# Decode attention on one core: q in one load, shared norms and stores, and the last V loads in pieces

## The chip, the cores and the metric

The kernel runs on one core of a Trainium2 chip. The metric is the device time in microseconds (us), lower is better. The profile adds a span, from the core's first to its last instruction, which lies 1.7 to 2.9 us under the device time. Where a reason is at stake I compare spans and times inside the trace; where a version is judged I compare device times.

## The reference, cut to what matters

```python
B, H, Sq, Skv, Dh = 8, 32, 1, 4096, 128          # bf16
def reference(q, k, v):
    scores = einsum('bhqd,bhkd->bhqk', q, k) * Dh ** -0.5
    attn = softmax(scores, axis=-1)
    return einsum('bhqk,bhkd->bhqd', attn, v)
```

There are 256 heads with one query each. K and V are 4096 x 128 per head, together 537 MB, and each number of them is used once.

## The kernel before

A "tile" t is four heads (G = 4). Its K is 4 MB, 128 partitions of 128 keys x 128 numbers, and so is its V; there are NT = 64 tiles. I write K63, V61 and so on for the K or V of a tile, and `av62` for the V product of tile 62. Per tile: VectorE multiplies K by q in place and folds it once; TensorE sums the rest over d by matmuls with the identity (`ps`); VectorE and ScalarE make the softmax weights `w`; TensorE multiplies `w` with V into `av`; four small matmuls bring `av` into shape (`op`); ScalarE scales by the norm `rz` into a staging tile, which is stored. The parts that the argument touches:

```python
    def load(kind, t):                       # five 4 MB slots for K and V together
        ...
        cuts = [C]
        if kind == "v" and t == NT - 1:
            cuts = [C // 2, C // 4, C // 8, C // 8]
        for n in cuts:
            nc.sync.dma_start(buf[:, c0 : c0 + n, :], src[t, :, c0 : c0 + n, :])
        ...
    def q_prep(t):
        if t % QN == 0:                      # every 4 tiles: 4 KB by POOL's queue
            nc.gpsimd.dma_start(qrow[:], q_g[:, t : t + QN, :])
            nc.tensor.matmul(qp[:], lhsT=sel[:], rhs=qrow..., start=True, stop=True)
            nc.scalar.activation(out=qb..., in_=qp[:], func=ACT.Copy)
    ...
    def values_of(t):
        nc.tensor.matmul(zp[:], lhsT=esum[:], rhs=ones[:], start=True, stop=True)
        nc.vector.reciprocal(out=rz[:], in_=zp[:])          # per tile
        for c0 in range(0, C, CB):
            nc.tensor.matmul(av[:], lhsT=w[:, c0 : c0 + CB, :], rhs=vt[:, c0 : c0 + CB, :], ...)
        nc.scalar.activation(out=comb[:], in_=av[:], func=ACT.Copy)
        for m in range(CB):
            nc.tensor.matmul(op[:], ...)
        nc.scalar.activation(out=stage[:, t % ON, :], in_=op[:], func=ACT.Copy, scale=rz[:, 0:1])
        ...                                                 # a store by POOL every 8 tiles

    for t in range(NT):
        ...                                  # loads of K(t+2) and V(t)
        product(t, 0, C // 2)
        if t > 0:
            weights_of(t - 1)
        product(t, C // 2, C)
        if t > 1:
            values_of(t - 2)
        sum_over_d(t)
    weights_of(NT - 1)
    values_of(NT - 2)
    values_of(NT - 1)
```

The framework that builds the kernel orders each engine's queue by its own estimate of when data arrive, so the queue need not follow the program text exactly. Each engine then works through its queue in order.

## Time and profile before

| | before |
|---|---|
| device time, median | 1269.99 us (three runs, 1269.97 to 1270.1) |
| span of the profiled run | 1268.9 us |
| a K or V tile lands every | 9.71 us |
| busy share DVE, PE, ACT | 74%, 67%, 14% |
| K63, V61, V62 and the last piece of V63 land at | 1226.5, 1236.2, 1245.9, 1255.7 us |

PE is TensorE, DVE VectorE, ACT ScalarE, POOL GpSimd, SP SyncE. A landing is the moment when the last of the 16 DMA engines of a load reports its share done; these moments are in the trace's semaphore records.

From the page of the kernel before, 40 equal slices of the span: the clock granted to TensorE and the busy share of the DMA engines, both in tenths, and the GB/s they moved.

```profile
PEclk9878988878888788888787887988878878889789
DMA  9999999999999999999999999999999999999994
GB/s 397 433 431 432 432 431 429 431 432 429 430 430 429 431 433 431 430 430 431 430 430 433 430 431 431 429 431 430 433 429 430 433 430 433 430 429 430 430 432 178
```

Every slice but the last moves 429 to 433 GB/s (397 in the first, with the start in it). The Trainium skill, page "DMA: Bandwidth & Descriptors", section "Where 436 GB/s comes from", gives 435.2 GB/s as the ceiling of one core; this trace comes within 1.5% of it. So there is next to no room in the middle of the kernel, and what may move is the head and the tail.

The waits of the kernel before say the same (engine, line, what it waited for: us in total, times, longest):

```profile
PE av L197 <- DMA vt<-in_v_dram: 349.0, 57, 7.9
DVE kt L132 <- DMA kt<-in_k_dram: 283.5, 57, 12.3
```

Now its tail, from the timeline (start us, duration us, engine, line, operation, output and inputs, count, and in brackets the idle time ahead of it and what ended that):

```profile
1226.50 4.49 DVE L132 TENSOR_TENSOR kt<-kt,qb 128x4096 bf16<-128x4096 bf16 x2 [4.78 <-DMA kt<-in_k_dram]
...
1236.23 10.02 PE L197 MATMUL av<-vt,w 128*16 128x512 bf16 x32 [5.83 <-DMA vt<-in_v_dram]
...
1246.18 1.04 PE L149 MATMUL ps<-kt,ident 128*128 128x512 bf16 x4
...
1247.14 0.38 PE L205 MATMUL op<-comb,ident 16*4 16x128 bf16 x4
...
1247.46 2.77 PE L149 MATMUL ps<-kt,ident 128*128 128x512 bf16 x12
...
1250.21 7.07 PE L197 MATMUL av<-vt,w 128*16 128x512 bf16 x32
...
1258.26 6.43 PE L197 MATMUL av<-vt,w 128*16 128x512 bf16 x29
...
1266.22 0.54 ACTq L216 DMA_DIRECT2D out_dram<-stage  x1
```

DVE starts on tile 63 when K63 has landed (1226.50). V61 lands whole at 1236.18 and releases av61 (32 matmuls, 10.02 us at a clock that is half at first). From there PE has no pause: sum of tile 63 (the `ps` rows), av62, av63 (its last 29 matmuls are the row at 1258.26). V63 has landed by 1255.7, yet the kernel runs to 1268.9. So the tail is a queue of PE work behind V61, not a wait for the last load.

### The profile page before, as it was taken

To read this page: it belongs to the slowest core of one execution; us is meant where nothing else is said; L and a number is where in the kernel's file an instruction comes from. 1 tells how busy PE (TensorE), PEld (TensorE's weight loads), DVE (VectorE), ACT (ScalarE), POOL (GpSimd) and SP (SyncE) were. 2 spreads that over 40 slices of the span, in tenths; PEclk is the share of its full clock that TensorE was granted. 3 is DMA by queue.
4 is the path that set the end of the run, shared out by engine and by line. 5 is a ranking of instruction groups with operands and counts; after the bars stand their busy time and mean duration, and the time that the engine had idled before them with its cause. 6 is when DMAs were issued, how large, how long until landed. Compare 5 with 4: busy or idle time off the path is not lost.

```text
span 1268.9 us, 9053 instructions
## 1 busy us (share of the span) xinstructions
PE 847.7 (67%) x3472; PEld 315.7 (25%) x3472; DVE 939.4 (74%) x898; ACT 181.7 (14%) x657; POOL 15.8 (1%) x36
## 2 busy tenths in 40 slices
PE   2548776766856767668577676676676866757668
PEld 0213222222322222223222222222222222222223
DVE  5869968677686686776866867768678677686771
ACT  0111110111111111111111011110111111101111
POOL 1000000000000000000000000000000000000000
PEclk9878988878888788888787887988878878889789
DMA  9999999999999999999999999999999999999994
GB/s 397 433 431 432 432 431 429 431 432 429 430 430 429 431 433 431 430 430 431 430 430 433 430 431 431 429 431 430 433 429 430 433 430 433 430 429 430 430 432 178
DMA packets 19683, 537.59 MB, mean 424 GB/s; under 512 B 2776, under 2 KB 2844, under 8 KB 3128
## 3 DMA queue, kind: packets, MB, share of 16 engines
q1 hardware_dynamic: 18864, 536.88, 98.5%
q8 instruction: 27, 0.44, 0.1%
q0 software_dynamic: 768, 0.14, 0.1%
q14 instruction: 16, 0.13, 0.0%
q10 hardware_dynamic: 8, 0.00, 0.0%
HBM read 536.94 MB, written 0.07 MB: 423 GB/s over the span
## 4 chain that ended last, share of the span: by engine, by line
DMA 69%; PE 25%; DVE 5%; ACT 0%; issue 0%; ACTq 0%; DVEq 0%
DMA vt<-in_v_dram 68%; PE av L197 24%; DVE kt L132 3%; DVE kt L135 1%; PE ps L149 1%; DMA kt<-in_k_dram 1%; ACT w L180 0%; DVE sc L159 0%; PE op L205 0%; ACT comb L202 0%; DVE pmax L163 0%; DVE spread L165 0%; DVE bias L174 0%; ACT qb L121 0%; PE qp L117 0%
## 5 line engine op out<-in xcount | busy, mean ns | idle before, releaser
L197 PE MATMUL av<-vt,w 128*16 128x512 bf16 x2048 | 573.8, 450 | 349.0 <-DMA vt<-in_v_dram 349.0
L132 DVE TENSOR_TENSOR kt<-kt,qb 128x4096 bf16<-128x4096 bf16 x256 | 579.4, 2285 | 283.5 <-DMA kt<-in_k_dram 283.5
L197 PEld LDWEIGHTS <-w 128*16 128x16 bf16 x2048 | 208.8, 102 | 696.4 <-issue 529.8
L135 DVE TENSOR_TENSOR kt<-kt 128x2048 bf16<-128x2048 bf16 x256 | 304.6, 1212 | 0.0
L149 PE MATMUL ps<-kt,ident 128*128 128x512 bf16 x1024 | 248.7, 385 | 24.0 <-DVE kt L135 24.0
L180 ACT ACTIVATE w<-sc,bias 128x128 bf16<-128x128 f32 x256 | 110.9, 567 | 697.1 <-DVE bias L174 697.1
L149 PEld LDWEIGHTS <-ident 128*128 128x128 bf16 x1024 | 89.6, 97 | 156.4 <-issue 58.9
L180 ACT ACTIVATION_READ_ACCUMULATOR w<-sc,bias 128x1 f32 x256 | 64.8, 253 | 0.0
L159 DVE TENSOR_REDUCE sc<-ps 128x128 f32<-128x512 f32 x64 | 43.8, 684 | 28.2 <-PE ps L149 28.2
L202 ACT ACTIVATE comb<-av 16x512 bf16<-16x512 f32 x64 | 37.6, 588 | 173.0 <-PE av L197 169.6
L121 ACT ACTIVATE qb<-qp 128x512 bf16<-128x512 f32 x16 | 9.6, 597 | 170.5 <-DVE kt L132 160.7
L212 ACT ACTIVATE stage<-op,rz 4x128 bf16<-4x128 f32 x64 | 22.9, 358 | 43.1 <-PE op L205 43.1
L205 PE MATMUL op<-comb,ident 16*4 16x128 bf16 x256 | 24.3, 213 | 5.9 <-ACT comb L202 5.9
L191 PE MATMUL zp<-ones,esum 128*4 128x1 f32 x128 | 12.3, 165 | 20.3 <-ACT w L180 20.3
L205 PEld LDWEIGHTS <-ident 16*4 16x4 bf16 x256 | 12.8, 78 | 33.0 <-issue 33.0
L117 PE MATMUL qp<-qrow,sel 4*128 4x512 bf16 x16 | 7.0, 436 | 18.9 <-DMA qrow<-in_q_dram 15.8
L163 DVE TENSOR_REDUCE pmax<-sc 128x1 f32<-128x128 f32 x64 | 17.9, 279 | 0.0
L115 POOL DMA_DIRECT2D qrow<-in_q_dram x16 | 9.3, 583 | 664.6 <-PE qp L117 664.6
L191 PEld LDWEIGHTS zp<-ones,esum 128*4 128x4 f32 x128 | 5.9, 84 | 46.9 <-issue 25.8
L165 DVE TENSOR_SCALAR spread<-zero,pmax 128x32 f32<-128x32 f32 x64 | 15.1, 235 | 0.1
L174 DVE TENSOR_SCALAR bias<-own,nmax 128x4 f32<-128x4 f32 x64 | 13.6, 212 | 0.0
L170 DVE TRANSPOSE_TENSOR_REDUCE nmax<-spread 128x1 f32<-128x32 f32 x64 | 13.1, 205 | 0.1
(18 smaller groups left out, 17.3 us busy)
## 6 DMA issues: line engine op xcount, KB each, us to landing
kt<-in_k_dram SPq DMA_DIRECT2D x64, 4096.0 KB, 35.5
vt<-in_v_dram SPq DMA_DIRECT2D x63, 4096.0 KB, 29.8
vt<-in_v_dram SPq DMA_DIRECT2D x1, 2048.0 KB, 24.5
vt<-in_v_dram SPq DMA_DIRECT2D x1, 1024.0 KB, 26.5
vt<-in_v_dram SPq DMA_DIRECT2D x2, 512.0 KB, 27.7
qrow<-in_q_dram POOLq DMA_DIRECT2D x16, 4.0 KB, 6.8
out_dram<-stage POOLq DMA_DIRECT2D x7, 8.0 KB, 6.7
out_dram<-stage POOLq DMA_DIRECT2D x1, 7.0 KB, 1.9
```

The lines of the kernel that those rows point to most:

```text
L132: nc.vector.tensor_tensor(out=part, in0=part, in1=qb[:, j : j + 1, :].to_broadcast([P, MC, D]), op=ALU.mult)
L135: nc.vector.tensor_tensor(out=part[:, :, 0 : D // 2], in0=part[:, :, 0 : D // 2], in1=part[:, :, D // 2 : D], op=ALU.add,)
L149: nc.tensor.matmul(ps[:], lhsT=ident[:], rhs=kt[:, u * UC : (u + 1) * UC, s * DS : (s + 1) * DS], start=(s == 0), stop=(s == n - 1),)
L159: nc.vector.tensor_reduce(out=sc[:, u * UC : (u + 1) * UC], in_=ps[:], axis=AX.X, op=ALU.add)
L163: nc.vector.tensor_reduce(out=pmax[:], in_=sc[:], axis=AX.X, op=ALU.max)
L165: nc.vector.tensor_scalar(out=spread[:], in0=zero[:], scalar1=pmax[:, 0:1], scalar2=-scale, op0=ALU.add, op1=ALU.mult,)
L180: nc.scalar.activation(out=w[:, :, g], in_=sc[:], func=ACT.Exp, bias=bias[:, g : g + 1], scale=scale, accum_out=esum[:, g : g + 1],)
L191: nc.tensor.matmul(zp[:], lhsT=esum[:], rhs=ones[:], start=True, stop=True)
L197: nc.tensor.matmul(av[:], lhsT=w[:, c0 : c0 + CB, :], rhs=vt[:, c0 : c0 + CB, :], start=(c0 == 0), stop=(c0 == C - CB),)
L202: nc.scalar.activation(out=comb[:], in_=av[:], func=ACT.Copy)
L205: nc.tensor.matmul(op[:], lhsT=ident[0 : CB * G, m * G : (m + 1) * G], rhs=comb[:, m * D : (m + 1) * D], start=(m == 0), stop=(m == CB - 1),)
L212: nc.scalar.activation(out=stage[:, t % ON, :], in_=op[:], func=ACT.Copy, scale=rz[:, 0:1])
```

## The change

Its intent: fetch q in one 64 KB load and spread it over partitions by matmuls; let four tiles (16 heads) share one PSUM tile, one norm, one reciprocal and one scaled copy, with fewer and larger stores, which ScalarE's queue issues instead of POOL's; and let the last three V loads arrive in pieces, so that TensorE can start on the first of them, with half of av62 ahead of the sum of tile 63. The diff, cut to its core:

```diff
+    q_all = consts.tile([NQ, R, G, D], BF16, name="q_all")
+    nc.scalar.dma_start(q_all.rearrange("n r g d -> n (r g d)"), q_n)
 ...
+    v_cuts = {
+        NT - 3: [C // 2] * 2,
+        NT - 2: [C // 4] * 4,
+        NT - 1: [C // 4] * 3 + [C // 8, C // 8],
+    }
 ...
-            nc.gpsimd.dma_start(qrow[:], q_g[:, t : t + QN, :])
-            nc.tensor.matmul(qp[:], lhsT=sel[:], rhs=qrow..., start=True, stop=True)
+            for g in range(G):
+                nc.tensor.matmul(
+                    qp[g * PH : (g + 1) * PH, :, :],
+                    lhsT=ident[0:NQ, n : n + 1].to_broadcast([NQ, PH]),
+                    rhs=q_all[:, :, g, :], start=True, stop=True,
+                )
 ...
+    def norm_of(n):                          # one zp matmul and one reciprocal for four tiles
+        nc.tensor.matmul(zp[:], lhsT=esums.pop(n).rearrange("p r g -> p (r g)"), rhs=ones[:], ...)
+        nc.vector.reciprocal(out=rzs[n][:], in_=zp[:])
+
+    def result_of(t):                        # op matmuls of four tiles into one [16, D] PSUM tile
+        n, r = divmod(t, R)
 ...
+                ops[n][:], lhsT=pick[:, m, r, :], rhs=comb[:, m * D : (m + 1) * D],
+                start=(r == 0 and m == 0), stop=(r == R - 1 and m == CB - 1),
+        if r < R - 1:
+            return                           # one scaled copy and, after 16 tiles, one store
 ...
-        sum_over_d(t)
-    weights_of(NT - 1)
-    values_of(NT - 2)
-    values_of(NT - 1)
+        if t < NT - 1:
+            sum_over_d(t)
+    values_of(NT - 2, 0, C // 2)
+    sum_over_d(NT - 1)
+    values_of(NT - 2, C // 2, C)
+    result_of(NT - 2)
+    weights_of(NT - 1)
+    norm_of(NQ - 1)
+    values_of(NT - 1, 0, C)
+    result_of(NT - 1)
```

More of the change, by code (lines that the diff above doesn't have):

```diff
@@ L15 @@
 SLOTS = 5
+R = 4
+OB = 4
 NEG = -1.0e30
@@ L41 @@
     MC = 32
-    QN = 512 // D
-    ON = 8
     CB = 4
-    q_g = q.rearrange("b h o d -> (b h o) d").rearrange("(t g) d -> g t d", g=G)
-    o_g = out.rearrange("b h o d -> (b h o) d").rearrange("(t g) d -> g t d", g=G)
+    RG = R * G
+    NQ = NT // R
+    assert NQ <= P and C % CB == 0
+    q_n = q.rearrange("b h o d -> (b h o d)").rearrange("(n x) -> n x", n=NQ)
+    o_n = out.rearrange("b h o d -> (b h o) d").rearrange("(n u x) d -> n x u d", u=OB, x=RG)
     k_t = k.rearrange("b h s d -> (b h s) d").rearrange("(t p c) d -> t p c d", p=P, c=C)
@@ L61 @@
     ps_z = ctx.enter_context(tc.tile_pool(name="ps_z", bufs=1, space=bass.MemoryType.PSUM))
-    sel = consts.tile([G, P], BF16, name="sel")
-    nc.gpsimd.memset(sel[:], 1.0)
-    nc.gpsimd.affine_select(
-        out=sel[:], in_=sel[:], pattern=[[1, P]], compare_op=ALU.is_ge,
-        fill=0.0, base=0, channel_multiplier=-PH,
-    )
-    nc.gpsimd.affine_select(
-        out=sel[:], in_=sel[:], pattern=[[-1, P]], compare_op=ALU.is_ge,
-        fill=0.0, base=PH - 1, channel_multiplier=PH,
-    )
+    q_all = consts.tile([NQ, R, G, D], BF16, name="q_all")
+    nc.scalar.dma_start(q_all.rearrange("n r g d -> n (r g d)"), q_n)
     ident = consts.tile([P, P], BF16, name="ident")
@@ L90 @@
     )
+    pick = consts.tile([CB * G, CB, R, RG], BF16, name="pick")
+    nc.gpsimd.memset(pick[:], 0.0)
+    nc.gpsimd.affine_select(
+        out=pick[:], in_=pick[:], pattern=[[-G, CB], [G, R], [-1, RG]],
+        compare_op=ALU.not_equal, fill=1.0, base=0, channel_multiplier=1,
+    )
+    nc.gpsimd.affine_select(
+        out=pick[:], in_=pick[:], pattern=[[-G, CB], [0, R], [0, RG]],
+        compare_op=ALU.is_ge, fill=0.0, base=0, channel_multiplier=1,
+    )
+    nc.gpsimd.affine_select(
+        out=pick[:], in_=pick[:], pattern=[[G, CB], [0, R], [0, RG]],
+        compare_op=ALU.is_ge, fill=0.0, base=G - 1, channel_multiplier=-1,
+    )
     zero = consts.tile([P, 32], F32, name="zero")
@@ L100, in load @@
         buf = kv_pool.tile([P, C, D], BF16, name=f"{kind}t", tag="kv")
-        cuts = [C]
-        if kind == "v" and t == NT - 1:
-            cuts = [C // 2, C // 4, C // 8, C // 8]
         c0 = 0
-        for n in cuts:
+        for n in v_cuts.get(t, [C]) if kind == "v" else [C]:
             nc.sync.dma_start(buf[:, c0 : c0 + n, :], src[t, :, c0 : c0 + n, :])
@@ L112, in q_prep @@
     def q_prep(t):
-        if t % QN == 0:
-            qrow = q_pool.tile([G, QN, D], BF16, name="qrow", tag="qrow")
-            nc.gpsimd.dma_start(qrow[:], q_g[:, t : t + QN, :])
-            qp = ps_q.tile([P, QN * D], F32, name="qp", tag="qp")
-            nc.tensor.matmul(
-                qp[:], lhsT=sel[:], rhs=qrow.rearrange("g n d -> g (n d)"), start=True, stop=True
-            )
-            qb = q_pool.tile([P, QN, D], BF16, name="qb", tag="qb")
-            nc.scalar.activation(out=qb.rearrange("p n d -> p (n d)"), in_=qp[:], func=ACT.Copy)
-            qbs[t // QN] = qb
-    state = {}
+        if t % R == 0:
+            n = t // R
+            qp = ps_q.tile([P, R, D], F32, name="qp", tag="qp")
+            for g in range(G):
[3 more added lines that the diff above has]
+                    rhs=q_all[:, :, g, :], start=True, stop=True,
+                )
+            qb = q_pool.tile([P, R, D], BF16, name="qb", tag="qb")
+            nc.scalar.activation(out=qb[:], in_=qp[:], func=ACT.Copy)
+            qbs[n] = qb
     def product(t, lo, hi):
         kt = loads["k", t]
-        qb = qbs[t // QN]
-        j = t % QN
+        qb = qbs[t // R]
+        j = t % R
         for c0 in range(lo, hi, MC):
@@ L154, in sum_over_d @@
             sums[t].append(ps)
+    ws = {}
+    esums = {}
     def weights_of(t):
@@ L177, in weights_of @@
         w = w_pool.tile([P, C, G], BF16, name="w", tag="w")
-        esum = small.tile([P, G], F32, name="esum", tag="esum")
+        if t % R == 0:
+            esums[t // R] = small.tile([P, R, G], F32, name="esum", tag="esum")
+        esum = esums[t // R]
         for g in range(G):
@@ L181, in weights_of @@
                 out=w[:, :, g], in_=sc[:], func=ACT.Exp, bias=bias[:, g : g + 1], scale=scale,
-                accum_out=esum[:, g : g + 1],
+                accum_out=esum[:, t % R, g : g + 1],
             )
-        state[t] = (w, esum)
-    stages = {}
-    def values_of(t):
-        w, esum = state.pop(t)
-        zp = ps_z.tile([G, 1], F32, name="zp", tag="zp")
-        nc.tensor.matmul(zp[:], lhsT=esum[:], rhs=ones[:], start=True, stop=True)
-        rz = small.tile([G, 1], F32, name="rz", tag="rz")
-        nc.vector.reciprocal(out=rz[:], in_=zp[:])
-        vt = loads.pop(("v", t))
-        av = ps_v.tile([CB * G, CB * D], F32, name="av", tag="av")
-        for c0 in range(0, C, CB):
+        ws[t] = w
@@ L197, in values_of @@
+    avs = {}
+    def values_of(t, lo, hi):
+        vt = loads["v", t]
+        w = ws[t]
+        if lo == 0:
+            avs[t] = ps_v.tile([CB * G, CB * D], F32, name="av", tag="av")
+        for c0 in range(lo, hi, CB):
             nc.tensor.matmul(
-                av[:], lhsT=w[:, c0 : c0 + CB, :], rhs=vt[:, c0 : c0 + CB, :],
+                avs[t][:], lhsT=w[:, c0 : c0 + CB, :], rhs=vt[:, c0 : c0 + CB, :],
                 start=(c0 == 0), stop=(c0 == C - CB),
             )
+    ops = {}
@@ L201, in values_of @@
+    rzs = {}
+    stages = {}
+    def norm_of(n):
+        zp = ps_z.tile([RG, 1], F32, name="zp", tag="zp")
+        nc.tensor.matmul(
+            zp[:], lhsT=esums.pop(n).rearrange("p r g -> p (r g)"), rhs=ones[:],
+            start=True, stop=True,
+        )
+        rzs[n] = small.tile([RG, 1], F32, name="rz", tag="rz")
+        nc.vector.reciprocal(out=rzs[n][:], in_=zp[:])
+    def result_of(t):
+        n, r = divmod(t, R)
         comb = small.tile([CB * G, CB * D], BF16, name="comb", tag="comb")
-        nc.scalar.activation(out=comb[:], in_=av[:], func=ACT.Copy)
@@ L203, in values_of @@
-        op = ps_o.tile([G, D], F32, name="op", tag="op")
+        nc.scalar.activation(out=comb[:], in_=avs.pop(t)[:], func=ACT.Copy)
+        if r == 0:
+            ops[n] = ps_o.tile([RG, D], F32, name="op", tag="op")
         for m in range(CB):
             nc.tensor.matmul(
-                op[:], lhsT=ident[0 : CB * G, m * G : (m + 1) * G],
-                rhs=comb[:, m * D : (m + 1) * D], start=(m == 0), stop=(m == CB - 1),
-            )
-        if t % ON == 0:
-            stages[t // ON] = o_pool.tile([G, ON, D], BF16, name="stage", tag="stage")
@@ L211, in values_of @@
-        stage = stages[t // ON]
-        nc.scalar.activation(out=stage[:, t % ON, :], in_=op[:], func=ACT.Copy, scale=rz[:, 0:1])
-        if t == NT - 1 or t == NT - 2 or (t % ON == ON - 1):
-            lo = {NT - 1: NT - 1, NT - 2: NT - ON}.get(t, t - ON + 1)
-            eng = nc.scalar if t == NT - 1 else nc.gpsimd
-            eng.dma_start(o_g[:, lo : t + 1, :], stage[:, lo % ON : t % ON + 1, :])
+                ops[n][:], lhsT=pick[:, m, r, :], rhs=comb[:, m * D : (m + 1) * D],
+                start=(r == 0 and m == 0), stop=(r == R - 1 and m == CB - 1),
+            )
@@ new lines, in result_of @@
+        if r < R - 1:
+            return
+        s, u = divmod(n, OB)
+        if u == 0:
+            stages[s] = o_pool.tile([RG, OB, D], BF16, name="stage", tag="stage")
+        nc.scalar.activation(
+            out=stages[s][:, u, :], in_=ops.pop(n)[:], func=ACT.Copy, scale=rzs.pop(n)[:, 0:1]
+        )
+        last = s == NQ // OB - 1
+        if u == OB - 1 or (last and u == OB - 2):
+            lo = u if (last and u == OB - 1) else 0
+            nc.scalar.dma_start(o_n[s, :, lo : u + 1, :], stages[s][:, lo : u + 1, :])
@@ L231 @@
         if t > 1:
-            values_of(t - 2)
-        sum_over_d(t)
+            values_of(t - 2, 0, C)
+            result_of(t - 2)
+            if (t - 2) % R == R - 2:
+                norm_of((t - 2) // R)
+        if t < NT - 1:
[4 more added lines that the diff above has]
+    result_of(NT - 2)
     weights_of(NT - 1)
-    values_of(NT - 2)
-    values_of(NT - 1)
+    norm_of(NQ - 1)
+    values_of(NT - 1, 0, C)
+    result_of(NT - 1)
 _INS = ['q', 'k', 'v']
```

## The prediction

> **What bounds it now.** The kernel streams 537 MB of K and V. The 40-slice rows show all DMA engines at 9 tenths in every slice but the last and 429 to 433 GB/s. The Trainium skill, "DMA: Bandwidth & Descriptors", section "Where 436 GB/s comes from", gives a ceiling of 435.2 GB/s for one core; the trace agrees to 1%. DVE (74%) and PE (67%) wait for data every tile: in the waits, PE's av matmuls waited 349 us for V, DVE's products 283 us for K. Loads are issued about 30 us before they land, so the queue never runs dry. A 4 MB tile lands every 9.71 us; 128 of them are 1243 us. The rest is a head (first K tile lands at 13.2 us) and a tail.
>
> **The tail (timeline from 1205 us).** K63 lands at 1226.5, V61 at 1236.2, V62 at 1245.9, the last piece of V63 at 1255.7; the span ends at 1268.9. After 1236.2 PE never rests: av61 10.0 us (half clock at first), the sum over d of tile 63 4.0 us, av62 7.1 us, av63 7.2 us, then comb, op, norm, store and end 4.2 us. So the last 13 us are queued PE work, not DMA.
>
> **What the change does.**
> - q: 16 loads of 4 KB from POOL become one of 64 KB. Matmuls 16 to 64 (436 ns each), hidden in PE's idle time. The first product waits for K0 at 13.2 us anyway. Worth 0.
> - Norms: zp matmuls 128 to 32, reciprocals and norm ACTIVATEs 64 to 16 each. About 48 x (0.36 + 0.25) = 29 us of ACT/PE/DVE busy time, all off the path. Worth 0, except that fewer small packets (the software queue took 13 us of packet time over 16 engines, under 1 us per engine) may let the slowest DMA engine end 0 to 0.5 us earlier.
> - Last V loads in pieces: av61 starts its first half at about 1231.3 instead of 1236.2 and ends near 1240.5 instead of 1246.2. But av62 needs the weights of tile 62, whose exponentials end at 1243.0 (DVE is busy with product 63 until 1241). So PE gains not 6 but about 3 us, with a short idle before 1243. Then half of av62 (3.6), sum 63 (4.0) to about 1250.7; other half of av62 to 1254.2; the weights of tile 63 take 3.9 us after the sum, about 1254.5; av63 7.1, end part 4.2: about 1266. The V63 pieces (last at 1255.7) are no longer what PE waits for, and weights 63 are just about the limit.
>
> **Prediction.** The span falls by 2 to 4 us in the tail alone: 1267.0 us, 80% range 1264.6 to 1269.3. Faster by over 2%: 0.01; within 2%: 0.98; slower by over 2%: 0.01.
>
> **What would show it.** Middle slices unchanged at 430 GB/s; ACT busy down by about 20 us with no effect; DMA bulk ending within 1 us of 1255; the PE idle of about 1236 moved earlier and split; span end minus last V landing about 10 us instead of 13.2; av62 beginning at about 1243, released by ACT w rather than by DMA.
>
> **What would make it wrong.** (a) The scheduler places sum 63 ahead of av62: weights 63 come early and the end is V63's landing plus a few us, 1263. (b) The new idle gaps make the PE clock fall to half (the skill, "TensorE: Matmul & The Clock Gate", Part 1; this trace shows 0.5 granted around 1235 to 1242 after a 6 us idle): up to 2 us lost in av62. (c) ACT's copies of av61 block PE's op matmuls in order. (d) The pieces or the stores on ACT's queue wait for one another and delay a load.

## The result, and the profile after

| | before | after |
|---|---|---|
| device time, median | 1270.05 us (4 runs) | 1268.97 us (4 runs, 1267.53 to 1269.94) |
| ratio, 95% interval | | 0.999 [0.9972, 1.0007] |
| span of the profiled run | 1268.9 us | 1267.1 us |
| instructions in the profile | 9053 | 8759 |
| K63, last of V63 land at | 1226.5, 1255.7 us | 1224.9, 1254.5 us |

A ratio is the mean time of one kernel's runs over that of the other's of the same rounds, so it is not quite the ratio of the medians quoted beside it. The time lies in the predicted range, 2 us above its centre. The interval of the ratio holds 1, so these four runs show no gain clear of noise (five more of the changed kernel, in e5, give 0.998 [0.9967, 0.9992]). The four runs spread over 2.4 us, which e5 takes up. The kernel before spreads as much, over 2.1 us in the nine runs beside e1 to e4 (1268.73 to 1270.86) and over 4.1 us in the nine beside e5 to e8, so a difference of 1 or 2 us between two profiled runs proves nothing by itself.

The same three rows of the page, kernel after:

```profile
PEclk9778878888879788888787887888877878888888
DMA  9999999999999999999999999999999999999994
GB/s 399 430 430 430 431 432 435 429 431 435 431 430 431 431 430 431 430 433 431 429 430 431 431 434 431 432 429 432 433 432 432 430 431 430 429 429 430 433 425 197
```

The middle is unchanged. The last slice moves a little more (197 instead of 178 GB/s), because it is a slice of a span whose end came nearer to the end of the loads.

The tail of the kernel after, from its timeline:

```profile
1224.89 4.49 DVE L144 TENSOR_TENSOR kt<-kt,qb 128x4096 bf16<-128x4096 bf16 x2 [4.81 <-DMA kt<-in_k_dram]
...
1229.81 3.62 PE L211 MATMUL av<-vt,w 128*16 128x512 bf16 x16 [1.05 <-DMA vt<-in_v_dram]
...
1234.73 3.61 PE L211 MATMUL av<-vt,w 128*16 128x512 bf16 x16 [1.31 <-DMA vt<-in_v_dram]
...
1239.44 0.38 PE L161 MATMUL ps<-kt,ident 128*128 128x512 bf16 x1 [1.09 <-DVE kt L147]
...
1241.35 1.45 PE L211 MATMUL av<-vt,w 128*16 128x512 bf16 x3 [1.53 <-ACT w L197]
...
1245.48 1.03 PE L161 MATMUL ps<-kt,ident 128*128 128x512 bf16 x2
1246.44 2.37 PE L211 MATMUL av<-vt,w 128*16 128x512 bf16 x8
...
1248.74 2.98 PE L161 MATMUL ps<-kt,ident 128*128 128x512 bf16 x13
...
1251.65 3.62 PE L211 MATMUL av<-vt,w 128*16 128x512 bf16 x16
...
1256.26 7.07 PE L211 MATMUL av<-vt,w 128*16 128x512 bf16 x32
...
1264.81 0.33 ACTq L251 DMA_DIRECT2D out_dram<-stage  x1
```

Four readings. K63 lands 1.6 us earlier (1224.89 against 1226.50), though the prediction allowed for half a microsecond at most. av61 runs in two halves and ends at 1238.35 instead of 1246.25, 2 us before the 1240.5 of the prediction. Then PE waits, and av62 starts at 1241.35, released by `ACT w`, the weights of tile 62, as predicted. But the first half of av62, with 2 `ps` and 4 `op` matmuls among it, takes from 1241.35 to 1248.74, where the next matmul starts: twice what was planned for it.

The windows of the kernel after show why (stretch, its length, busy time and instruction counts of each engine, then the clock granted to TensorE, DMA share, GB/s):

```profile
1239.00:1241.00 2.00, 0.38 (x1) 0.00 (x0) 0.53 (x2) 1.44 (x7) 0.00 (x0) 0.90 0.99 414
1241.00:1243.00 2.00, 1.65 (x6) 0.52 (x7) 0.00 (x0) 0.72 (x3) 0.00 (x0) 0.50 1.03 430
1243.00:1245.00 2.00, 2.00 (x8) 0.54 (x6) 0.00 (x0) 0.00 (x0) 0.00 (x0) 0.50 0.99 412
1245.00:1247.00 2.00, 2.00 (x6) 0.37 (x5) 0.00 (x0) 0.00 (x0) 0.00 (x0) 0.50 0.99 408
1247.00:1249.00 2.00, 2.00 (x10) 0.64 (x8) 0.00 (x0) 0.00 (x0) 0.00 (x0) 0.89 0.68 283
```

The clock is 0.50 from 1240.6 to 1247.4 (the trace's clock records give these two moments). In 1243 to 1247 PE was busy all the time and finished 14 matmuls.

The chain that ended last has another root as well (start, duration, what). Before, its last long DMA piece was V61; after, it is K63:

```profile
1206.37 29.81 DMA vt<-in_v_dram
```

```profile
1188.82 36.04 DMA kt<-in_k_dram
```

Once V61's pieces no longer hold PE up, what holds it up is the way from K63 through DVE's product and ACT's exponentials to `w`.

### The profile page after: what moved, and what is told of

It reads as the page before. It is cut to its first block, busy times and chain, and to the rows that moved or that the text cites. A ratio compares the mean times of both kernels' runs of the same rounds, so it can differ in the third digit from the quotient of the medians.

```text
span 1267.1 us, 8759 instructions
## 1 busy us (share of the span) xinstructions
PE 848.8 (67%) x3424; PEld 316.9 (25%) x3424; DVE 939.4 (74%) x850; ACT 164.0 (13%) x609; POOL 2.7 (0%) x13
## 4 chain that ended last, share of the span: by engine, by line
DMA 67%; PE 24%; DVE 7%; ACT 1%; issue 0%; DVEq 0%; ACTq 0%
DMA vt<-in_v_dram 63%; PE av L211 22%; DVE kt L144 4%; DMA kt<-in_k_dram 4%; DVE kt L147 2%; PE ps L161 2%; ACT w L197 1%; DVE sc L174 0%; PE op L236 0%; ACT comb L232 0%; DVE pmax L178 0%; DVE bias L189 0%; DVE spread L180 0%; DVE nmax L185 0%; PE zp L222 0%
## 5 line engine op out<-in xcount | busy, mean ns | idle before, releaser
L161 PE MATMUL ps<-kt,ident 128*128 128x512 bf16 x1024 | 254.3, 391 | 33.4 <-DVE kt L147 33.4
L236 PE MATMUL op<-comb,pick 16*16 16x128 bf16 x256 | 25.2, 219 | 5.3 <-ACT comb L232 5.3
L236 PEld LDWEIGHTS <-pick 16*16 16x16 bf16 x256 | 13.8, 85 | 33.0 <-issue 33.0
L129 PE MATMUL qp<-q_all,ident 16*32 16x512 bf16 x64 | 7.6, 430 | 21.3 <-ACT qb L135 14.9
L222 PE MATMUL zp<-ones,esum 128*16 128x1 f32 x32 | 3.1, 166 | 8.3 <-ACT w L197 8.3
L245 ACT ACTIVATE stage<-op,rz 16x128 bf16<-16x128 f32 x16 | 5.7, 357 | 10.7 <-PE op L236 10.7
```

The source lines that it names most:

```text
L161: nc.tensor.matmul(ps[:], lhsT=ident[:], rhs=kt[:, u * UC : (u + 1) * UC, s * DS : (s + 1) * DS], start=(s == 0), stop=(s == n - 1),)
L236: nc.tensor.matmul(ops[n][:], lhsT=pick[:, m, r, :], rhs=comb[:, m * D : (m + 1) * D], start=(r == 0 and m == 0), stop=(r == R - 1 and m = ...
```

## The experiments

Two theories to start with. A: the end is set by PE's chain; the pieces shorten it, and the half clock, and perhaps the new order with half of av62 ahead of the sum of tile 63, give it back. B: the pieces do little, and the 1.8 us come from the earlier landing of K63. All kernels gave correct results. The four kernels e1 to e4 ran on one chip with 9 runs of the kernel before (median 1269.71), e5 to e8 with 9 others (1270.21), e9 to e11 with 7 (1269.88).

### e1: the pieces alone

```diff
 # on the kernel before
-        if kind == "v" and t == NT - 1:
-            cuts = [C // 2, C // 4, C // 8, C // 8]
+        if kind == "v":
+            cuts = {
+                NT - 3: [C // 2] * 2,
+                NT - 2: [C // 4] * 4,
+                NT - 1: [C // 4] * 3 + [C // 8, C // 8],
+            }.get(t, [C])
```

> The kernel before with only the new cuts of the last three V loads; q, outputs, norms and the order of the tail stay as before (there TensorE does the whole sum of tile 63 ahead of av62). Theory A (the end is set by TensorE's chain from K63, and the cuts alone free it): K63 lands at 1226.5 us as before, av61 ends about 1239.8 instead of 1246.2, the sum of tile 63 ends about 1246.6 because its op of tile 61 waits for the exponentials of 62 (1243), av63 ends about 1261; span 1265.3, that is 3.6 us under before. Rival B (the gain of 1.8 us in the span comes from q and the outputs, through earlier landings of K63): no gain, span within 0.5 us of 1268.9.

Measured: span 1265.7 in the profiled run, device time 1267.98 us (median of 5; before 1269.71). The ratio to before is 0.9995 [0.9982, 1.0007]: no gain clear of noise. Three of its spans are 1265.7 to 1266.2 and two 1268.9 and 1269.0. From its timeline:

```profile
1235.92 3.61 PE L201 MATMUL av<-vt,w 128*16 128x512 bf16 x16 [1.29 <-DMA vt<-in_v_dram]
1240.68 1.03 PE L153 MATMUL ps<-kt,ident 128*128 128x512 bf16 x4 [1.14 <-DVE kt L139]
1243.07 0.38 PE L209 MATMUL op<-comb,ident 16*4 16x128 bf16 x4 [1.36 <-ACT comb L206]
1243.38 2.77 PE L153 MATMUL ps<-kt,ident 128*128 128x512 bf16 x12
...
1246.13 7.07 PE L201 MATMUL av<-vt,w 128*16 128x512 bf16 x32
...
1254.18 7.07 PE L201 MATMUL av<-vt,w 128*16 128x512 bf16 x32
```

av61 ends at 1239.5, the sum of tile 63 at 1246.1, av63 at 1261.2: A's numbers. The pieces alone move the profiled span by 3.2 us, more than the whole change did in its profiled run. In this run B's "no gain" does not hold. Part of it is the clock, though: here it was full from 1220.6 to 1265.0, and the 32 matmuls of av61 took 3.61 + 3.61 us instead of 10.02. That two of five runs lost 3 us again was not expected, and they have no trace.

### e2: the sum of tile 63 first

```diff
 # on the changed kernel
-        if t < NT - 1:
-            sum_over_d(t)
-    values_of(NT - 2, 0, C // 2)
-    sum_over_d(NT - 1)
-    values_of(NT - 2, C // 2, C)
-    result_of(NT - 2)
-    weights_of(NT - 1)
+        sum_over_d(t)
+    weights_of(NT - 1)
+    values_of(NT - 2, 0, C)
+    result_of(NT - 2)
```

> The changed kernel, but with the old order of the tail: the sum of tile 63 ahead of all of av62. Theory A (the split put the sum of tile 63, which the last weights hang on, behind half of av62, and that gives back part of what the cuts gained): the sum ends near 1246 instead of 1251.7, av62 runs through to about 1253, the last weights are ready in time, av63 ends near 1260.5; span 1264.4, 2 to 4 us under the changed kernel's 1267.1. Rival C (the split helps as it was meant to, because half of av62 fills TensorE's wait): span 1268 or more.

Measured: span 1263.7 in the profiled run (1263.7 to 1264.1 in four of five, 1265.4 in the other), device time 1265.68 us, ratio to before 0.9971 [0.9958, 0.9985]. C's 1268 or more did not come. But A's reason is not shown by this run: the clock was full from 1219.4 to the end in its trace, so order and clock changed together. e4 separates them.

### e3: the old pieces under the new order

The changed kernel with V61 and V62 whole and V63 in its old four pieces. Without further care the framework, which expects V62 later then, moves the sum of tile 63 forward; so PE's tail is pinned matmul by matmul to the changed kernel's order.

```diff
 # on the changed kernel, PE's tail pinned
     v_cuts = {
-        NT - 3: [C // 2] * 2,
-        NT - 2: [C // 4] * 4,
-        NT - 1: [C // 4] * 3 + [C // 8, C // 8],
+        NT - 1: [C // 2, C // 4, C // 8, C // 8],
     }
```

> The changed kernel with V61 and V62 whole and V63 in the old four pieces; TensorE's order is pinned to exactly the changed kernel's. Theory A: V61 is whole at 1234.7 plus some skew, about 1237, av61 ends near 1245 to 1246 at a partly halved clock, everything after it follows, span 1268.7 or so, 1 to 2 us over the changed kernel. Rival B (the pieces do nothing here, the chain from K63 alone sets the end, as the chain view shows DMA of K63 as its root): the same span as the changed kernel within 0.5 us.

Measured: spans 1267.0 to 1267.3 in all five runs, device time 1269.01 us. That is not A's 1268.7; it is within 0.1 us of the changed kernel's profiled span, 1267.1, so B's number was right here. From its timeline:

```profile
1234.45 9.37 PE L226 MATMUL av<-vt,w 128*16 128x512 bf16 x32 [6.50 <-DMA vt<-in_v_dram]
...
1244.17 0.81 PE L226 MATMUL av<-vt,w 128*16 128x512 bf16 x3
...
1251.68 3.62 PE L226 MATMUL av<-vt,w 128*16 128x512 bf16 x16
```

av61 starts when the whole of V61 has landed (1234.41) and ends at 1243.8 instead of 1238.4. But it took the half clock in av61 (1232.3 to 1239.1 in the clock records), and from av62 on it ran at full clock and without a wait: it starts av62 2.8 us after the changed kernel and starts the second half of av62 at the same time, 1251.7. So in the changed kernel's profiled run the pieces were worth nothing. Whether they are worth something when the clock is full, e4 and e5 tell.

### e4: keep TensorE busy in its wait

```diff
 # on the changed kernel, PE's tail pinned
+    warm = ps_q.tile([P, R, D], F32, name="warm", tag="qp")
+    for i in range(12):                      # between av61 and the sum of tile 63; results unused
+        nc.tensor.matmul(warm[:], lhsT=ident[:], rhs=loads["v", NT - 3][:, 0:CB, :],
+                         start=True, stop=True)
```

> The changed kernel with its TensorE order pinned and 12 matmuls of no use between av61 and the sum of tile 63, where TensorE waited 3 us (1238.35 to 1241.35); results are unchanged. Theory A (the half clock granted from 1240.6 to 1247.4 cost about 2.5 us of the predicted gain): clock stays full in that stretch, the 16 av62, 3 sum and 4 op matmuls of it take 4.5 instead of 7.4 us, span about 1264.6. Rival D (that stretch is slow for its waits and switches between chains, not for its clock): the same span as the changed kernel, or longer by what the fillers delay.

Measured: spans 1264.0 to 1264.7 in all five runs, device time 1266.04 us (1265.76 to 1266.4), ratio 0.9972 [0.996, 0.9985]. From its windows, the stretches shown above for the kernel after:

```profile
1239.00:1241.00 2.00, 1.96 (x10) 0.68 (x7) 0.25 (x2) 1.72 (x9) 0.00 (x0) 1.00 1.01 422
1241.00:1243.00 2.00, 1.92 (x11) 0.76 (x12) 0.00 (x0) 0.45 (x3) 0.00 (x0) 1.00 1.02 426
1243.00:1245.00 2.00, 2.00 (x10) 0.64 (x9) 0.00 (x0) 0.00 (x0) 0.00 (x0) 1.00 0.99 412
1245.00:1247.00 2.00, 2.00 (x11) 0.72 (x10) 0.00 (x0) 0.00 (x0) 0.00 (x0) 1.00 1.02 420
```

The clock stays at 1.00. From 1241 to 1247 it is 32 matmuls instead of 20, and the same first half of av62 with its `op` and `ps` matmuls ends at 1245.7 instead of 1248.7. Useless matmuls made the kernel 3.1 us shorter than the changed kernel's profiled run. Against e3 (1267.0, same order, old pieces) the pieces are worth 3.0 us. Not all of that is the earlier start: e3's av61 took 9.37 us, partly at half clock, where the kernel before takes 7.07 us for the 32 matmuls of av62 at full clock. So, as an estimate from these figures, 2.3 of the 3.0 us are the half clock that e3 had in av61 and e4 had nowhere; an e3 at full clock was not run. And as its order is the changed kernel's and e2's is the old one, 1264.0 against 1263.7 leaves 0.3 us for the order at full clock. So the new order as such costs next to nothing; the clock does.

### e5: the changed kernel again

> The changed kernel itself once more, beside the others of this call. If the clock grant falls by chance into the stretch from av61's end to the sum of tile 63 (theory A), its spans spread over 2 us or so, 1264.5 to 1268, with the profiled trace at the lower end when the clock is full from 1240 to 1247 and at 1267 when it is half there. Rival: the spans are tight and the clock in that stretch is half every time.

Measured: spans 1264.3, 1264.5, 1264.7, 1265.9 and 1267.3; the profiled run was the 1267.3 one, and its clock was half from 1240.8 to 1247.6. Device time 1267.63 us (before 1270.21), ratio 0.998 [0.9967, 0.9992]. The three fast ones agree with e4, whose profiled run had the full clock. Of the nine runs of the changed kernel in all, three are at 1264.3 to 1264.7 and six at 1265.8 to 1268.1. The two with a trace, both slow, show the half clock in the same place. The other four slow ones have only a mean clock for the whole span (0.837 to 0.85), so that it was the same half clock in them too is likely, not shown.

In the device times of this kernel there is also 1.7 to 2.9 us outside the span, where the other kernels have 1.7 to 2.1; that stays unexplained.

### e6 and e7: why does K63 land earlier?

e6 is the kernel before with the new q alone; e7 is the changed kernel with the old q loads. The theory I held (Q) was the prediction's: fewer small packets on the DMA engines.

```diff
 # e6, on the kernel before
-            nc.gpsimd.dma_start(qrow[:], q_g[:, t : t + QN, :])
-            nc.tensor.matmul(qp[:], lhsT=sel[:], rhs=qrow..., start=True, stop=True)
+    (q_all by one load, and four spreading matmuls, as in the change)
 # e7, on the changed kernel
-    (q_all and the spreading matmuls)
+    (the 16 loads by POOL's queue and the matmul with sel, as before)
```

> The kernel before with the new q alone: one 64 KB load and the spreading matmuls; outputs, cuts and order as before. Theory Q (without 16 small loads of the software queue every DMA engine has less to do, so K63 lands at 1225.3 or earlier instead of 1226.1 to 1226.5, though K0 lands 0.5 us later): span about 1 us under before. Rival O (the stores did it, or the head start): K63 lands at 1226 or later, span as before.

> The changed kernel with the old q loads; the shared PSUM tile, norms, stores, cuts and order as changed. Theory Q: K63 lands at about 1225.7 instead of 1224.9 and the span is about 1 us over the changed kernel's at the same clock. Rival O: K63 lands as in the changed kernel, 1224.9 or earlier, and the span is the same.

The start of DVE's work on tile 63, which K63's landing releases, in e6 and in e7:

```profile
1227.26 4.49 DVE L128 TENSOR_TENSOR kt<-kt,qb 128x4096 bf16<-128x4096 bf16 x2 [4.76 <-DMA kt<-in_k_dram]
```

```profile
1224.97 4.49 DVE L149 TENSOR_TENSOR kt<-kt,qb 128x4096 bf16<-128x4096 bf16 x2 [4.86 <-DMA kt<-in_k_dram]
```

Theory Q fell, in both. With the new q alone K63 lands at 1227.2, 0.8 us later than before; with the old q and all the rest of the change it lands at 1224.95, like the changed kernel. (Medians: e6 1269.12 us, span 1267.1 to 1268.9; e7 1268.24 us, span 1266.1 to 1267.4.) e1, which has the cuts alone, has K63 at 1226.1, so it is in the outputs' part. But not in its packets: the DMA queues' records sum to 13.0 us of packet time for the software queue before, spread over 16 engines, and in e7, where K63 lands early, that queue still has 7.4 us.

The landings themselves gave the lead. Take the difference of each tile's landing from the one before, less 9.71 us. It is near zero but for single jumps, and from 390 us on the jumps stand in step with 8 KB reads of an instruction queue (q14):

```
before   8 KB read at   393.9  550.5  707.0  863.5 1020.0 1176.4   (every 156 us)
         landing jumps  +1.27  +0.79  +1.03  +1.14  +1.01  +0.98   at 396, 552, 708, 865, 1021, 1178
after    8 KB read at   432.7  608.5  784.3  960.1 1136.0          (every 176 us)
         landing jumps  +1.02  +0.93  +1.01  +1.02  +1.01          at 434, 610, 786, 962, 1137
```

Between two such reads VectorE ran 128 instructions in every interval before (394 to 550.5, to 707, to 863.5) and 128 or 129 after, and no other engine's count fits (ScalarE: 91 before; SyncE: 32). Before, VectorE had 16 instructions a tile, so 128 were 8 tiles; without the reciprocal of every tile and what it waits on, 128 are 9 tiles. The Trainium skill, page "Runtime: NRT & Kernel Launch", section "Instruction fetch mechanics", says that a sequencer fetches its program by DMA on a queue of its own while it executes. Theory V: each fetch of VectorE's program goes through one DMA engine that also carries K and V, always the same one, and sets it back by 1 us; a tile counts as landed only when its slowest engine is done. Why a read that itself took 0.32 us costs 1 us stays open.

One limit of this lead has to be said. e1 and e6 run the VectorE program of the kernel before, yet most of their larger jumps are not at its reads. They stand at 123, 484 and 855 us in e1 and at 125, 427, 788 and 1159 us in e6, each 5 to 9 us after a 16 KB read of the other instruction queue, q8 (117, 477 and 848 us; 116, 421, 782 and 1154 us). There another engine was the slowest. VectorE's fetches move a landing only where their engine is the last one.

### e9 and e10: put VectorE instructions back

```diff
 # on the changed kernel; N = 2 in e9, N = 16 in e10
         product(t, C // 2, C)
+        for i in range(N):
+            tc.keep_in_program_order(nc.vector.memset(scrap[:], 0.0))     # [128, 1], never read
```

> The changed kernel with two tiny VectorE memsets per tile of no use, which brings VectorE's program back to about 16 instructions a tile, as before. Theory V (K63 lands 1.5 us earlier in the changed kernel because VectorE has fewer instructions: an 8 KB piece of its program is fetched every 128 instructions, by one of the DMA engines that carry K and V, and each fetch sets that engine back by about 1 us; in the trace the landings jump by 1 us just where VectorE's fetches stand, every 156 us before and every 176 us after): one fetch more by K63, which lands at about 1226 instead of 1224.9; jumps every 156 us. Rival S (the stores' or the norm's own data traffic made the difference): K63 lands at 1224.9 plus or minus 0.3.

> The same with 16 memsets per tile, 1024 instructions or about 8 fetches of VectorE's program more; VectorE's own time grows by about 1 us a tile, within the 3 to 4 us it waits for K. Theory V: K63 lands about 8 us later than in the changed kernel, near 1232 to 1233, with jumps of 1 us every 80 to 85 us, and the span is about 1273 to 1275. Rival S: K63 lands at 1225 and the span stays at 1264.5 to 1267.5.

The page's line for that instruction queue (packets, MB, share) in the changed kernel, then in e9 with DVE's start on tile 63 from its timeline, then the same two for e10 (the changed kernel's start, 1224.89, is shown above):

```profile
q14 instruction: 14, 0.11, 0.0%
```

```profile
q14 instruction: 15, 0.12, 0.0%
```

```profile
1226.02 4.49 DVE L145 TENSOR_TENSOR kt<-kt,qb 128x4096 bf16<-128x4096 bf16 x2 [4.67 <-DMA kt<-in_k_dram]
```

```profile
q14 instruction: 22, 0.18, 0.0%
```

```profile
1232.83 4.49 DVE L145 TENSOR_TENSOR kt<-kt,qb 128x4096 bf16<-128x4096 bf16 x2 [2.92 <-DMA kt<-in_k_dram]
```

Theory V holds. Counted by VectorE's instructions, 8 KB reads of its program by the time K63 lands are 8 before, 7 after, 8 in e9 and 15 in e10. Two useless instructions a tile bring K63 back to 1226.0, with jumps every 156 us from 376 to 1002 us; sixteen bring it to 1232.8, 7.9 us later, with jumps of 0.8 to 1.0 us that come every 78 to 89 us from 201 us on. The DMA engines that finish first finish K63 at 1217.4 in e10 and at 1217.6 in the changed kernel; only the slowest moves. And VectorE isn't the limit: the sixteen took 1.97 us a tile, twice what I expected, and it still waited 2.92 us for K63. e10's device time is 1274.76 us, 0.3% over before (ratio 1.0033 [1.0016, 1.005]). e9's is 1268.75 us; its span, 1267.0, hides the later landing, because in its profiled run the half clock lasted 3.4 us and not 6.8.

### e8 and e11: a better version

If the chain from K63 is what holds PE up, K63 should come in pieces as well, and the sum of tile 63 should go ahead of av62.

```diff
 # e8, on the changed kernel, PE's tail pinned to:
 #   av61, sum 63, op61, av62, half of av63, op62, other half of av63
+        k_cuts = {NT - 1: [MC] * 4}
-        NT - 1: [C // 4] * 3 + [C // 8, C // 8],
+        NT - 1: [C // 4] * 3 + [C // 8, C // 16, C // 16],
 # e11, on e8: products in blocks of 64 keys
+        mc = MC if t == NT - 1 else 2 * MC
```

> The changed kernel with K63 in four pieces as well, V63's last eighth in two, and TensorE's tail pinned: av61, the whole sum of 63, op61, av62, half of av63, op62, the rest. Theory A: the product of tile 63 starts near 1220 instead of 1224.9 and ends near 1235, the sum follows av61 at 1238.3 to 1242, av62 ends near 1249.5, the weights of 63 are ready at 1246, and av63 waits for the pieces of V63, the last at 1254.3; span 1259.5, about 5 us from the last landing, and 9 us under before. Rival (the tail is set by what follows V63's landing or by SyncE's many issues): span 1262 or more.

> The kernel of e8_k_pieces with the products in blocks of 64 keys instead of 32 (not in tile 63), which takes four VectorE instructions a tile away. Theory V: VectorE's fetches come every 240 us or so, two fewer by the end; the DMA engine that was last gains up to 2 us, until another one (those that fetch TensorE's program) is last: V63 lands at 1253 to 1254 instead of 1254.8, span 1259 to 1260 instead of 1260.6. Rival S: no change of the landing; span within 0.4 us of 1260.6.

e8: spans 1260.6 to 1260.8, device time 1262.41 us (1262.37 to 1262.53), ratio to before 0.9939 [0.9925, 0.9952]. It beats both kernels, and five runs agree within 0.2 us. What each of its three edits (K63's pieces, V63's smaller last pieces, the order) gave was not separated. From its timeline:

```profile
1235.01 3.61 PE L229 MATMUL av<-vt,w 128*16 128x512 bf16 x16 [1.26 <-DMA vt<-in_v_dram]
1238.56 3.63 PE L167 MATMUL ps<-kt,ident 128*128 128x512 bf16 x16
...
1242.44 7.07 PE L229 MATMUL av<-vt,w 128*16 128x512 bf16 x32
...
1253.26 3.62 PE L229 MATMUL av<-vt,w 128*16 128x512 bf16 x16
```

The sum of tile 63 follows av61 without a pause, and the clock is full from 1220.4 to the end. The span is 1.1 us over my 1259.5: PE is busy from V61's second half (1235.0) to the end of av63 (1256.9) and does not wait for V63 (last piece 1254.8), as I had expected it to.

e11: VectorE's program has 667 instructions instead of 920, five fetches by K63 instead of seven, and the last piece of V63 lands 0.96 us earlier than in e8 (1253.84), as theory V has it; that two fetches fewer gave 1 us and not 2 fits another DMA engine being the last by then, for the jumps left stand at 434, 814 and 1185 us and not at VectorE's fetches. The time is the same: 1262.12 us against 1262.41, spans 1259.9 to 1261.0. In its profiled run the last store was issued 1.03 us earlier than in e8, at 1257.33, and its last packet ran late: 15 of the 16 packets were written by 1258.33, the last at 1258.96 to 1258.98, after a 16 KB instruction read that started at 1257.98 and took 0.98 us. So in this run an instruction fetch seems to have taken back what fewer fetches had given; one trace with the two side by side is all there is for it. The other three spans, 1259.9 to 1260.4, are 0.2 to 0.9 us under e8's.

## Why the prediction was right or wrong

The range and the "within 2%" held, and the main mechanism was right. Two terms of the sum were wrong in size, with opposite signs, and partly cancelled; that the number came so near owes something to this luck.

- **The middle is bound by DMA; q is worth 0.** Right. The slices are unchanged, and e6 shows no gain from q. A detail was missed: the first product starts at 13.79 instead of 13.28 us with the new q, for K0 lands half a microsecond later.
- **"The slowest DMA engine [may] end 0 to 0.5 us earlier", from fewer small packets.** Mis-sized and wrongly reasoned. K63 landed 1.6 us and V63 1.2 us earlier. e6 and e7 show that q's packets did not do it; e9 and e10 show that VectorE's shorter program did, by one instruction fetch of 1 us less. That covers 1.1 of the 1.6 us (e9 against the changed kernel); the rest, 0.5 us, is within what other kernels with the same VectorE program differ by (1226.1 to 1227.2 among before, e1 and e6).
- **"av61 ... ends near 1240.5", "av62 needs the weights of tile 62, whose exponentials end at 1243.0".** Right, less the 1.6 us by which K63 came earlier: 1238.35 and 1241.3. The release by ACT was named in advance and seen.
- **"Half of av62 (3.6)".** This term was mis-sized. It took 7.4 us in the profiled run, 1241.35 to 1248.74, with the small matmuls among it; in e4 the same work at full clock took 4.6 us, of which about 1 us is the small matmuls that the 3.6 left out. The prediction named this risk as (b), up to 2 us; it cost 2.8 us of this stretch, and 3.1 us of the span against e4. It strikes some runs and not others, and it strikes the kernel before too, but there in av61, for which 10.0 us were read from the trace with the half clock already in it.
- **"About 1266" for the span.** With the half clock the changed kernel ends at 1267.1 or 1267.3 (the two traces); without it, most likely, at the 1264.3 to 1264.7 of its three fast runs, which have no trace. (The other four, 1265.8 to 1268.1, fit neither and have no trace either.) The predicted span lies between the two.
- **"Span end minus last V landing about 10 us".** Wrong: 12.6 us, for the same reason; in e4 it is 9.8 (1264.0 less 1254.2).
- **(a), the sum of tile 63 ahead of av62: "the end is ... 1263".** It did not happen in the change; e2 made it so and measured 1263.7. But the reason given for it is not what mattered: at full clock the two orders differ by 0.3 us.

Where did the gain of the pieces go? When the clock stays full they are worth 3.0 us (e4 against e3), and by the estimate above most of that is the half clock itself: with V61 whole, PE waits about 6 us for it, and av61 then runs partly at half clock (10.02 us before, 9.37 in e3, against 7.07 at full clock). In the profiled run of the change the half clock fell into av62 instead, on the path as well, and took it all back.

What stays open: what decides whether a run meets the half clock at that place (e2, with waits much like the changed kernel's, met a long span once in five, the changed kernel six times in nine), and the time outside the span.

## What to carry to other kernels

When loads bind a kernel, look at the tail as a queue: find which landing its last unbroken run of TensorE work hangs on, and cut that load, here K63 as well as V61. When you free an engine from one wait, check the TensorE clock in the new gaps and, if it falls, fill them or reorder so that none are left. And count instructions even on an engine with time to spare: its program comes through the same DMA engines as the data, and a stream at its ceiling pays 1 us for each fetch that meets its slowest engine. In device time this showed only in e10, with 16 instructions a tile and 0.3%.

## What the Trainium skill lacked or had wrong

- "Runtime: NRT & Kernel Launch", section "Instruction fetch mechanics", says that crossing a block boundary is mostly hidden. For the engine that executes, nothing here contradicts it: in the kernel before, every wait of VectorE over 0.3 us was ended by a load or by another engine. But it lacks what a fetch does to others: where the engine that fetches VectorE's program was the slowest of a saturated stream, each 8 KB fetch set the landings back by about 1 us (jumps of 0.8 to 1.3 us in the kernel before from 390 us on; 16 more instructions a tile moved a landing by 7.9 us). In e11 the last packet of a store was written 0.6 us after the others, just when a 16 KB read ended.
- The same section gives blocks of 16 KiB, 256 instructions, for the engines. VectorE's came as 8 KB reads, one for every 128 instructions; only the other instruction queue (27 packets of 16 KB) had the size of the page.
- "TensorE: Matmul & The Clock Gate", section "Why this matters for your kernels", advises gaps of no more than about 3 us between bursts. Here the clock fell to half at 1240.6 us although the three gaps between matmuls since 1228 had been 1.05 to 1.31 us and the fourth had lasted 0.8 us by then. Such gaps don't always do it: e2 had four of 1.12 to 1.59 us and kept the full clock. (The page itself tells of a clock lost to short idles between groups of matmuls, but gives no length for them.) Its Part 1 says that the clock is judged in free-running windows of 3.4 us; the lengths seen here (6.8 and, in e9, 3.4 us of half clock) agree, as does a spread from run to run.
- "DMA: Bandwidth & Descriptors", section "Where 436 GB/s comes from", says that for loads from HBM about 358 GB/s bind. Taken alone that misleads: one core alone read at 423 GB/s over the whole span here, near the page's ceiling of 435.2 and its own 425 for one core whose neighbour is idle.
- That a load is complete only when all its engines have reported stands in "DMA: Bandwidth & Descriptors". What no page gives is how far apart the engines can drift in a long stream: here the first and the last were 0.5 us apart at the first tile and 8.1 us apart at K63 before, and the kernel waits for the last.
